# Both scaled copies of the token mixing on VectorE, and a longer TensorE delay in the list scheduler's model

## The chip, the core and the metric

The kernel runs on one core of one Trainium2 chip. The metric is the device time of one execution in microseconds, the median of three runs. TensorE multiplies matrices, VectorE and ScalarE do elementwise work, GpSimd here only writes zeros, and SyncE issues every DMA. Each of them works through its own list of instructions in order; only semaphores tie them together.

## What is computed

The reference, cut to its core: an attention with a sigmoid in place of the softmax, then a channel mixing on its output. The sizes are B = 8, 12 heads, S = 448 tokens, 64 values a head, so D = 768, and 1024 hidden values. All of it is in fp32.

```
scores = q @ k.T / sqrt(64) - log(S)
x      = sigmoid(scores) @ v                  # heads joined: (B, S, 768)
x_prev = x shifted by one token, zero in front
xk = mu_k * x + (1 - mu_k) * x_prev
xr = mu_r * x + (1 - mu_r) * x_prev
k  = relu(xk @ w_k)
out = sigmoid(xr @ w_r) * ((k * k) @ w_v)
```

## The kernel before

**Attention (lines 297 to 349).** Two heads make one tile of 128 partitions, and there are 48 tiles. Two tiles are worked on together; such a pair is called a round here, and there are 24. A round has 7 steps, one for each block of 64 keys. In a step TensorE makes a score group (`score`, line 317: eight matmul rows in the trace, into the PSUM buffer `sc`, of which there are two), ScalarE turns it into weights with one sigmoid over 128 x 896 (line 320, into `pf`, three buffers), and TensorE multiplies the weights of two steps earlier with the values (`weigh`, line 329, eight rows, into `av`). On TensorE the list runs: score group, weighing group two steps behind, next score group, and so on. A score group writes the `sc` buffer that the sigmoid of two steps earlier has read. There are four `av` banks, two for a round, so a round's banks are written again two rounds later.

**Mixing (`gather`, lines 334 to 349).** After the last weighing of a round, each of its two tiles is mixed twice, for `xr` and for `xk`. GpSimd writes the zero in front. One engine writes the scaled copy `(1 - mu) * x_prev`, reading `av`: VectorE for `xr` (line 345, `omr`), ScalarE for `xk` (line 347, `omk`). VectorE adds `mu * x` (line 348), reading `av` again, and SyncE stores the 128 x 448 result `xo`, of which there are eight buffers. A round so has two copies on VectorE, two on ScalarE and four sums on VectorE.

**Weights (lines 200 to 291).** The weights arrive as 64-bit floats, and VectorE turns them into fp32 with integer operations (lines 212 to 216), then forms the sums and differences that a seven-product (Strassen) scheme needs (line 244). For `w_r` ScalarE casts each piece into a weight slot (line 289, `slot`) and VectorE makes the remainder (line 290). This runs in the first ten rounds of the attention. The pieces of `w_k` go back to DRAM and are cast later (lines 515 and 516).

**Channel mix (lines 351 to 612).** Three linear maps, each in four halves of the tokens and seven products p, in the order 0, 1, 4, 5, 6, 2, 3. Each product is made of three partial products of high and low parts (line 530). Its operands are split by a cast on ScalarE (line 413) and a difference on VectorE (line 414), some after differences of their own (line 407). Products go to the PSUM banks `xb` (p = 0, 1, 4, 2) or `yb` (5, 6, 3); sums on VectorE read them (lines 568, 573, 574, 578, 582).

**What sets the order.** Nothing is written in engine order by hand. Every operation is handed to a `Plan` with its engine, a cost in ns, a due time and the buffers that it reads and writes. `Plan.order` then plays the engines through: an engine takes, of the operations that are ready, the one with the earliest due time. An operation is ready when those that it depends on have ended, plus `WAIT` = 170 ns, or plus 0 between two TensorE operations. `emit` issues the operations by the start times found. There are two plans, one up to the end of the attention and one for the channel mix. The scheduler's times are its own; only the order gets into the program.

Of the kernel before, what the change touches and what calls it, by code (L numbers as in the profile page):

```python
# [22 lines left out]
class Plan:  # L23
# [7 lines left out]
    def op(self, engine, cost, prio, run, reads, writes, dma=None):  # L31
        i = len(self.ops)
        deps = set()
        for r in reads:
            if r in self.writer:
                deps.add(self.writer[r])
        for w in writes:
            if w in self.writer:
                deps.add(self.writer[w])
            deps.update(self.readers.get(w, ()))  # L40
        for r in reads:
            self.readers.setdefault(r, []).append(i)
        for w in writes:
            self.writer[w] = i
            self.readers[w] = []
        deps.discard(i)
        self.ops.append(Op(engine, cost, prio, run, deps, dma))

    def order(self):
        import heapq  # L50
        ops = self.ops
        left = [len(o.deps) for o in ops]
        users = [[] for _ in ops]
        for i, o in enumerate(ops):
            for d in o.deps:
                users[d].append(i)
        at = [0.0] * len(ops)
        free, ready, waiting = {}, {}, []
        for i, o in enumerate(ops):
            free[o.engine] = 0.0  # L60
            ready.setdefault(o.engine, [])
            if not left[i]:
                heapq.heappush(waiting, (0.0, i))
        bus, start = self.bus, {}
        now = 0.0
        while len(start) < len(ops):
            while waiting and waiting[0][0] <= now:
                i = heapq.heappop(waiting)[1]
                heapq.heappush(ready[ops[i].engine], (ops[i].prio, i))
            for e in free:  # L70
                if free[e] <= now and ready[e]:
                    i = heapq.heappop(ready[e])[1]
                    o = ops[i]
                    start[i] = now
                    free[e] = now + o.cost
                    end = now + o.cost
                    if o.dma is not None:
                        bus = max(bus, end + 700) + o.dma
                        end = bus + 1300
                    for u in users[i]:  # L80
                        gap = 0 if ops[u].engine == e == "PE" else self.WAIT
                        at[u] = max(at[u], end + gap)
                        left[u] -= 1
                        if not left[u]:
                            heapq.heappush(waiting, (at[u], u))
            nxt = [free[e] for e in free if ready[e]] + ([waiting[0][0]] if waiting else [])
            if nxt:
                now = max(now, min(nxt)) if min(nxt) > now else now
        self.start = start
        return sorted(start, key=lambda i: (start[i], i))  # L90
# [8 lines left out]
def attention_then_channel_mix(  # L99
# [15 lines left out]
    nc = tc.nc  # L115
# [32 lines left out]
    xr_d = [dram.tile([P, NJ, S], F32, name=f"xr_d{b}") for b in range(B)]  # L148
# [33 lines left out]
    op = plan.op  # L182
    SP, PE, ACT, DVE, POOL = "SP", "PE", "ACT", "DVE", "POOL"
# [4 lines left out]
    def act(n, sbuf=False, ptr=False):  # L188
        return 51 + 0.834 * n + 42 * sbuf + 93 * ptr

    def dve(n, fast=False, ptr=False):
        return 69 + n / (1.92 if fast else 0.96) + 61 * ptr
# [7 lines left out]
    def dma(dst, src, prio, reads, writes):  # L200
        ns = dst.shape[0] * math.prod(dst.shape[1:]) * 4 / 300
        op(SP, 500, prio, lambda: nc.sync.dma_start(dst, src), reads, writes, dma=ns)
# [119 lines left out]
    def bank(m):  # L322
        return m % 4
# [12 lines left out]
    def gather(n, at):  # L336
        b, j = divmod(n, NP)
        x, X = av[bank(n)], ("av", bank(n))
        for mu, om, dst, key in ((mur, omr, xr_d, "xr_d"), (muk, omk, xk_d, "xk_d")):
            u = nxo[0] % len(xo)  # L340
            nxo[0] += 1
            y, Y = xo[u], ("xo", u)
            op(POOL, 200, at, lambda y=y: nc.gpsimd.memset(y[:, 0:1], 0.0), [], [Y])
            if key == "xr_d":
                op(DVE, dve(S, ptr=True), at, lambda y=y, om=om: nc.vector.tensor_scalar_mul(y[:, 1:], x[:, :S - 1], om[:, j:j + 1]), [X, ("om", key)], [Y])  # L345
            else:
                op(ACT, act(S, ptr=True), at, lambda y=y, om=om: nc.scalar.mul(y[:, 1:], x[:, :S - 1], om[:, j:j + 1]), [X, ("om", key)], [Y])  # L347
            op(DVE, dve(S, ptr=True), at, lambda y=y, mu=mu: nc.vector.scalar_tensor_tensor(y, x[:, :S], mu[:, j:j + 1], y, ALU.mult, ALU.add), [X, Y], [Y])  # L348
            dma(dst[b][:, j], y, at, [Y], [(key, n)])

# [109 lines left out]
    for t in range(T + LAG):  # L460
        n, j = t // NV * 2, t % NV
        if t < T:
            if j == 0:
                for _ in range(1 + (n % 6 == 4)):
                    convert_next(n + 4, n - 2 if n else None)
            score(n, j, t, n + j / NV)
        if t < LAG:
            continue
        n, j = (t - LAG) // NV * 2, (t - LAG) % NV
        weigh(n, j, t - LAG, n + j / NV)  # L470
        if j == NV - 1:
            for m in (n, n + 1):
                gather(m, m)
                if m + 4 < N:
                    load(m + 4, n + 0.5)
# [22 lines left out]
    op = plan.op  # L498
# [89 lines left out]
    at = 0  # L588
# [49 lines left out]
```

## Time and profile before

| | |
|---|---|
| median of three runs | 824.85 us (824.68 to 825.09) |
| the profiled execution | 824.86 us |
| its span, first to last instruction | 823.1 us |
| granted TensorE clock | 0.999 of full |
| busy: TensorE, VectorE, ScalarE | 99%, 75%, 57% of the span |
| first product of the channel mix | 263.7 us from the span's start |

The span has two parts: the attention up to 263.7 us, in which the matmuls are small and every step needs a sigmoid, and the channel mix, in which TensorE runs long products. In the profile a row gives the instructions of one kind, `x` and their count; PE is TensorE, DVE VectorE, ACT ScalarE, SPq SyncE's queue. What stands in brackets in a timeline row is the engine's idle time ahead of it and what ended that. A row with `x2` merges two instructions that follow each other.

### The profile page before, as it was taken

The numbers are of one execution on the slowest core, as the hardware profiler recorded it, in microseconds if no ns is written. First come the engines' busy times: TensorE is split into PE (matmuls) and PEld (weight loads), VectorE is DVE, ScalarE is ACT, GpSimd is POOL, SyncE is SP. The second block draws the span as 40 slices with busy tenths as digits, with TensorE's granted clock in tenths as the row PEclk, the third lists the DMA queues.
The fourth block names the chain that finished last, engine by engine and source line by source line (L and its number), as shares of the span: only waits on it lengthen the run. The fifth ranks groups of instructions, "written<-read, shape, count | busy, mean of one in ns | idle before, by whom it ended". The sixth has DMA issues, their size and how long they took to land.

```text
span 823.1 us, 15181 instructions
## 1 busy us (share of the span) xinstructions
PE 812.9 (99%) x5460; PEld 622.9 (76%) x5460; DVE 615.1 (75%) x1152; ACT 467.1 (57%) x791; POOL 10.3 (1%) x100
## 2 busy tenths in 40 slices
PE   8999999999999999999999999999999999999997
PEld 3433334343334999999999999999999999999997
DVE  0888687685654898989999639376697795977955
ACT  5788776767676553546584747647694233333320
POOL 0000000000000000000000000000000000000000
PEclk9999999999999999999999999999999999999999
DMA  8787789999872948576879542422865545755414
GB/s 274 267 312 265 268 272 317 335 352 308 287 262 90 304 161 264 169 247 206 328 228 316 195 146 102 151 96 102 288 217 188 164 145 190 225 179 178 143 39 156
DMA packets 94715, 179.80 MB, mean 218 GB/s; under 512 B 10544, under 2 KB 75312, under 8 KB 94640
## 3 DMA queue, kind: packets, MB, share of 16 engines
q1 hardware_dynamic: 94640, 178.83, 64.7%
q8 instruction: 43, 0.70, 0.4%
q14 instruction: 32, 0.26, 0.1%
HBM read 109.06 MB, written 69.73 MB: 217 GB/s over the span
## 4 chain that ended last, share of the span: by engine, by line
PE 90%; DVE 4%; ACT 2%; DMA 2%; issue 1%; SPq 0%; ACTq 0%; DVEq 0%
PE xb L530 39%; PE yb L530 29%; PE sc L317 12%; PE av L329 11%; DVE xo L348 1%; ACT pf L320 1%; DMA raw<-in_qk 1%; ACT xo L347 1%; DMA wraw<-in_moe_w_r 1%; DVE wbit L216 0%; DVE wbit L215 0%; DVE wbit L214 0%; DVE xo L345 0%; DMA wk_o<-wbit 0%; DVE wbit L244 0%
## 5 line engine op out<-in xcount | busy, mean ns | idle before, releaser
L530 PE MATMUL xb<-rra,slot 128*128 128x448 f32 x1188 | 249.8, 362 | 0.0
L530 PEld LDWEIGHTS xb<-rra,slot 128*128 128x128 f32 x1188 | 222.7, 188 | 15.5 <-issue 0.7
L530 PE MATMUL yb<-rra,slot 128*128 128x448 f32 x927 | 193.0, 362 | 0.0
L320 ACT ACTIVATE pf<-sc 128x896 f32<-128x896 f32 x168 | 152.1, 918 | 58.9 <-PE sc L317 58.8
L530 PEld LDWEIGHTS yb<-rra,slot 128*128 128x128 f32 x927 | 173.8, 187 | 11.6
L317 PE MATMUL sc<-raw 64*64 64x448 f32 x1344 | 165.6, 545 | 5.4 <-DMA raw<-in_qk 3.5
L329 PE MATMUL av<-pf,vn 64*64 64x448 f32 x1344 | 162.3, 537 | 0.0
L317 PEld LDWEIGHTS sc<-raw 64*64 64x64 f32 x1344 | 52.0, 134 | 84.9 <-issue 57.0
L329 PEld LDWEIGHTS av<-pf,vn 64*64 64x64 f32 x1344 | 54.0, 133 | 74.9 <-issue 73.6
L530 PE MATMUL xb<-rrb,slot 128*128 128x448 f32 x396 | 89.1, 362 | 0.0
L345 DVE TENSOR_SCALAR xo<-av,omr 128x447 f32<-128x447 f32 x48 | 32.5, 681 | 73.6 <-PE av L329 47.1
L413 ACT CAST rra<-ysa 128x448 fp32r<-128x448 f32 x104 | 56.6, 562 | 50.5 <-PE yb L530 21.9
L530 PEld LDWEIGHTS xb<-rrb,slot 128*128 128x128 f32 x396 | 74.2, 187 | 5.0
L414 DVE TENSOR_TENSOR rra<-ysa,rra 128x448 fp32r<-128x448 f32 x102 | 59.6, 617 | 10.4 <-ACT rra L413 10.3
L530 PE MATMUL yb<-rrb,slot 128*128 128x448 f32 x261 | 57.5, 362 | 0.0
L530 PEld LDWEIGHTS yb<-rrb,slot 128*128 128x128 f32 x261 | 48.9, 187 | 3.3
L413 ACT CAST rra<-ysb 128x448 fp32r<-128x448 f32 x58 | 31.4, 564 | 34.2 <-PE yb L530 19.2
L568 DVE TENSOR_TENSOR u<-yb,p1s 128x448 f32<-128x448 f32 x40 | 24.9, 622 | 30.5 <-PE yb L530 30.1
L566 ACT COPY p1s<-xb 128x448 f32<-128x448 f32 x40 | 21.2, 530 | 39.9 <-PE xb L530 39.5
L413 ACT CAST rra<-wbit 128x448 fp32r<-128x448 f32 x46 | 24.4, 566 | 29.7 <-PE yb L530 29.1
L414 DVE TENSOR_TENSOR rra<-ysb,rra 128x448 fp32r<-128x448 f32 x54 | 31.4, 617 | 13.0 <-ACT rra L413 13.0
L548 ACT ACTIVATE cc<-cc 128x448 f32<-128x448 f32 x48 | 27.5, 577 | 19.8 <-DVE cc L574 13.5
(59 smaller groups left out, 712.9 us busy)
## 6 DMA issues: line engine op xcount, KB each, us to landing
k_d<-cc SPq DMA_DIRECT2D x64, 224.0 KB, 2.1
raw<-in_qk SPq DMA_DIRECT2D x48, 256.0 KB, 4.1
vn<-in_v SPq DMA_DIRECT2D x48, 224.0 KB, 5.3
xr_d<-xo SPq DMA_DIRECT2D x48, 224.0 KB, 3.5
xk_d<-xo SPq DMA_DIRECT2D x48, 224.0 KB, 3.4
r_d<-cc SPq DMA_DIRECT2D x48, 224.0 KB, 2.0
out<-cc SPq DMA_DIRECT2D x48, 224.0 KB, 3.1
raw<-in_qk SPq DMA_DIRECT2D x48, 192.0 KB, 4.5
```

What stands on the lines that cost most here:

```text
L317: nc.tensor.matmul(u[half[h ^ (m % 2)], m % 2, :S], x[half[h], c], x[half[h], D:D + S], start=True, stop=True)
L320: op(ACT, act(2 * S), at, lambda: nc.scalar.activation(f, u[:, :, :S], AF.Sigmoid, bias=NEG_LOG_S, scale=SCALE), [("sc", t % 2)], [("pf", ...
L329: nc.tensor.matmul(av[bank(m)][half[r ^ (m % 2)], :S], vn[m % RAW][half[r], j, :], pf[t % PFB][half[r], m % 2, :], start=j == 0, stop=j == ...
L345: op(DVE, dve(S, ptr=True), at, lambda y=y, om=om: nc.vector.tensor_scalar_mul(y[:, 1:], x[:, :S - 1], om[:, j:j + 1]), [X, ("om", key)], [Y])
L347: op(ACT, act(S, ptr=True), at, lambda y=y, om=om: nc.scalar.mul(y[:, 1:], x[:, :S - 1], om[:, j:j + 1]), [X, ("om", key)], [Y])
L348: op(DVE, dve(S, ptr=True), at, lambda y=y, mu=mu: nc.vector.scalar_tensor_tensor(y, x[:, :S], mu[:, j:j + 1], y, ALU.mult, ALU.add), [X, ...
L413: op(ACT, act(TB, True), at, lambda t=t: nc.scalar.copy(hi[t], y[:, t]), [Y[t]], [H[t]])
L414: op(DVE, dve(TB), at, lambda t=t: nc.vector.tensor_sub(lo[t], y[:, t], hi[t]), [Y[t], H[t]], [L[t]])
L530: nc.tensor.matmul(bank, a, b, start=first and t == 0 and e == 0, stop=t == n - 1 and e == 2, skip_group_check=True)
L548: op(ACT, act(TB), at, lambda: nc.scalar.activation(c, src, AF.Relu), R, [C])
L566: op(ACT, act(TB), at, lambda: nc.scalar.copy(p1s[i], x), [X], [P1])
L568: op(DVE, dve(TB), at, lambda: add(u2[i], y, p1s[i]), [Y, P1], [U2])
```

## The change

It has two parts. In `gather` the scaled copy for `xk` goes to VectorE as well, so that both copies are made there and ScalarE makes none. In `Plan.order` the delay from a TensorE operation to one on another engine becomes 370 ns; all others stay at 170, and 0 between TensorE operations.

```diff
                     for u in users[i]:
-                        gap = 0 if ops[u].engine == e == "PE" else self.WAIT
+                        gap = 0 if ops[u].engine == e == "PE" else self.WAIT + 200 * (e == "PE")
                         at[u] = max(at[u], end + gap)
...
             op(POOL, 200, at, lambda y=y: nc.gpsimd.memset(y[:, 0:1], 0.0), [], [Y])
-            if key == "xr_d":
-                op(DVE, dve(S, ptr=True), at, lambda y=y, om=om: nc.vector.tensor_scalar_mul(y[:, 1:], x[:, :S - 1], om[:, j:j + 1]), [X, ("om", key)], [Y])
-            else:
-                op(ACT, act(S, ptr=True), at, lambda y=y, om=om: nc.scalar.mul(y[:, 1:], x[:, :S - 1], om[:, j:j + 1]), [X, ("om", key)], [Y])
+            op(DVE, dve(S, ptr=True), at, lambda y=y, om=om: nc.vector.tensor_scalar_mul(y[:, 1:], x[:, :S - 1], om[:, j:j + 1]), [X, ("om", key)], [Y])
             op(DVE, dve(S, ptr=True), at, lambda y=y, mu=mu: nc.vector.scalar_tensor_tensor(y, x[:, :S], mu[:, j:j + 1], y, ALU.mult, ALU.add), [X, Y], [Y])
```

TensorE's and GpSimd's lists stay the same, row for row. On VectorE, ScalarE and SyncE instructions change places. In the changed kernel line numbers from 345 on are three lower: the copies are line 344, the sums 345, the operand splits 410 and 411, the slot additions 513, the sums of products 570, 571 and 575.

VectorE, the first round's mixing, before (`xo` are the mixed rows, `omr` and `omk` the two 1 - mu, `mur` and `muk` the two mu, `wbit` and `wexpo` the weight conversion that follows):

```order
L345 TENSOR_SCALAR xo0_156<-av0_135,omr_65 128x447
L345 TENSOR_SCALAR xo2_158<-av1_136,omr_65 128x447
L348 SCALAR_TENSOR_TENSOR xo0_156<-av0_135,mur_63,xo0_156 128x448
L348 SCALAR_TENSOR_TENSOR xo1_157<-av0_135,muk_64,xo1_157 128x448
L348 SCALAR_TENSOR_TENSOR xo2_158<-av1_136,mur_63,xo2_158 128x448
L348 SCALAR_TENSOR_TENSOR xo3_159<-av1_136,muk_64,xo3_159 128x448
L212 TENSOR_SCALAR wbit_127<-wraw_126 128x384
```

The same place now:

```order
L344 TENSOR_SCALAR xo0_156<-av0_135,omr_65 128x447
L344 TENSOR_SCALAR xo1_157<-av0_135,omk_66 128x447
L345 SCALAR_TENSOR_TENSOR xo0_156<-av0_135,mur_63,xo0_156 128x448
L345 SCALAR_TENSOR_TENSOR xo1_157<-av0_135,muk_64,xo1_157 128x448
L344 TENSOR_SCALAR xo2_158<-av1_136,omr_65 128x447
L344 TENSOR_SCALAR xo3_159<-av1_136,omk_66 128x447
L345 SCALAR_TENSOR_TENSOR xo2_158<-av1_136,mur_63,xo2_158 128x448
L345 SCALAR_TENSOR_TENSOR xo3_159<-av1_136,muk_64,xo3_159 128x448
L212 TENSOR_SCALAR wbit_127<-wraw_126 128x384
```

The two copies for `xk` stand among VectorE's own, and one tile is finished before the other is begun.

ScalarE, the first casts of weight pieces, in the second and third round, before (`pf` are the sigmoids, `slot` the cast pieces):

```order
L320 ACTIVATE pf1_154<-sc1_140 128x896
L289 CAST slot6_122<-wbit_127 128x384
L320 ACTIVATE pf2_155<-sc0_139 128x896
L289 CAST slot2_118<-wbit_127 128x384
L320 ACTIVATE pf0_153<-sc1_140 128x896
L347 ACTIVATE xo5_161<-av2_137,omk_66 128x447
L347 ACTIVATE xo7_163<-av3_138,omk_66 128x447
L320 ACTIVATE pf1_154<-sc0_139 128x896
```

The same place now, as far as the casts of the following round:

```order
L320 ACTIVATE pf2_155<-sc0_139 128x896
L289 CAST slot6_122<-wbit_127 128x384
L289 CAST slot2_118<-wbit_127 128x384
L320 ACTIVATE pf0_153<-sc1_140 128x896
...
L320 ACTIVATE pf2_155<-sc0_139 128x896
L289 CAST slot0_116<-wbit_127 128x384
L320 ACTIVATE pf0_153<-sc1_140 128x896
L289 CAST slot3_119<-wbit_127 128x384
L289 CAST slot4_120<-wbit_127 128x384
L320 ACTIVATE pf1_154<-sc0_139 128x896
L289 CAST slot1_117<-wbit_127 128x384
```

The copies are gone, and the first two casts stand together behind one sigmoid, one sigmoid later than the first of them stood.

VectorE, the product p = 6 in the last half of the first linear map, before (`cc` are the sums that read the banks `yb` and `xb`, `slot` an addition for the next map's weights, `rra` and `ysa` operands):

```order
L573 TENSOR_TENSOR cc4_2485<-yb0_2494,p1s0_2473 128x448
L414 TENSOR_TENSOR rra_124<-ysa_125,rra_124 128x448
L574 TENSOR_TENSOR cc4_2485<-xb0_2498,cc4_2485 128x448
L573 TENSOR_TENSOR cc0_2481<-yb1_2495,p1s1_2474 128x448
L516 TENSOR_TENSOR slot2_118<-wc2_2488,slot2_118 128x384
L574 TENSOR_TENSOR cc0_2481<-xb1_2499,cc0_2481 128x448
```

The same place now:

```order
L570 TENSOR_TENSOR cc4_2485<-yb0_2494,p1s0_2473 128x448
L411 TENSOR_TENSOR rra_124<-ysa_125,rra_124 128x448
L571 TENSOR_TENSOR cc4_2485<-xb0_2498,cc4_2485 128x448
L404 TENSOR_TENSOR ysa_125<-ysb_2472,ysa_125 128x448
L513 TENSOR_TENSOR slot2_118<-wc0_2486,slot2_118 128x384
L513 TENSOR_TENSOR slot2_118<-wc1_2487,slot2_118 128x384
L570 TENSOR_TENSOR cc0_2481<-yb1_2495,p1s1_2474 128x448
L570 TENSOR_TENSOR cc1_2482<-yb2_2496,p1s2_2475 128x448
L571 TENSOR_TENSOR cc0_2481<-xb1_2499,cc0_2481 128x448
```

A difference and two slot additions stand between the first row's sums and the second row's, which then wait behind the third row's first sum.

## The prediction

> **What bounds the kernel now.** I read the page first, for the busiest engine.
>
> ```profile
> PE 812.9 (99%) x5460; PEld 622.9 (76%) x5460; DVE 615.1 (75%) x1152; ACT 467.1 (57%) x791; POOL 10.3 (1%) x100
> ```
>
> TensorE is busy for 812.9 of 823.1 us, so the change can only pay or cost through TensorE's own schedule. A busy row hides stretched groups, so next I read the chain of waits in order of time. Its pieces give the start and length of TensorE's groups: `sc` is a score group, `xb` and `yb` are the products of the channel mix.
>
> ```profile
> 34.64 0.75 PE sc L317 x8
> ...
> 46.40 0.75 PE sc L317 x8
> ...
> 69.70 0.75 PE sc L317 x8
> ...
> 95.66 0.80 PE sc L317 x8
> ...
> 111.41 0.75 PE sc L317 x8
> ...
> 201.61 0.80 PE sc L317 x8
> ...
> 217.03 0.75 PE sc L317 x8
> ...
> 247.10 0.85 PE sc L317 x8
> ...
> 263.73 16.41 PE xb L530 x81
> 280.14 10.80 PE yb L530 x54
> ...
> 811.14 7.22 PE yb L530 x36
> ```
>
> One step is a score group and a weighing group. From 111.41 to 201.61 there are 60 steps in 90.20 us, 1.5033 us each, with no stall. The other distances are whole steps plus a loss: 34.64 to 46.40 is 7 steps and 1.24 us; to 69.70 is 15 steps and 0.75; to 95.66 is 17 and 0.40; to 111.41 is 10 and 0.72; 201.61 to 217.03 is 10 and 0.39; to 247.10 is 20 and nothing, but that row is 0.85 long, 0.10 over. From 263.73 to 818.36 (811.14 + 7.22) the products follow each other; what stands behind, 4.7 us, is the last sums and the last store.
>
> Who held the late score groups shows in the timeline of ScalarE. `pf` is the sigmoid that TensorE waits for, `xo` a scaled copy, `slot` a weight cast; the brackets hold the idle time before a row and what ended it.
>
> ```profile
> 26.04 0.92 ACT L320 ACTIVATE pf<-sc 128x896 f32<-128x896 f32 x1 [0.59 <-PE sc L317]
> ...
> 30.89 1.16 ACT L347 ACTIVATE xo<-av,omk 128x447 f32<-128x447 f32 x2 [0.40 <-DVE xo L345]
> ...
> 34.02 0.92 ACT L320 ACTIVATE pf<-sc 128x896 f32<-128x896 f32 x1 [0.35 <-PE sc L317]
> ...
> 41.34 0.91 ACT L320 ACTIVATE pf<-sc 128x896 f32<-128x896 f32 x1
> 42.58 1.22 ACT L347 ACTIVATE xo<-av,omk 128x447 f32<-128x447 f32 x2 [0.33 <-DVE xo L345]
> 43.70 0.91 ACT L320 ACTIVATE pf<-sc 128x896 f32<-128x896 f32 x1
> ...
> 64.45 1.16 ACT L347 ACTIVATE xo<-av,omk 128x447 f32<-128x447 f32 x2 [0.54 <-DVE xo L345]
> ...
> 91.95 1.11 ACT L289 CAST slot<-wbit 128x384 fp32r<-128x384 f32 x2 [0.91 <-DVE wbit L216]
> ...
> 106.86 0.91 ACT L320 ACTIVATE pf<-sc 128x896 f32<-128x896 f32 x1
> ...
> 108.69 0.93 ACT L320 ACTIVATE pf<-sc 128x896 f32<-128x896 f32 x1
> ...
> 213.28 1.16 ACT L347 ACTIVATE xo<-av,omk 128x447 f32<-128x447 f32 x2 [0.86 <-DVE xo L345]
> ...
> 223.79 1.16 ACT L347 ACTIVATE xo<-av,omk 128x447 f32<-128x447 f32 x2 [0.46 <-DVE xo L345]
> 224.84 1.72 ACT L320 ACTIVATE pf<-sc 128x896 f32<-128x896 f32 x2
> ...
> 244.94 1.16 ACT L347 ACTIVATE xo<-av,omk 128x447 f32<-128x447 f32 x2 [0.56 <-DVE xo L345]
> ```
>
> 26.04 to 34.02 is 5 steps and 0.46 us, behind the copies at 30.89. So the losses after the start sum to 0.46 + 1.24 + 0.75 + 0.40 + 0.72 + 0.39 + 0.10 = 4.06 us. Copies alone stand ahead of 0.46, 0.75 (64.45), 0.39 (213.28) and 0.10 (244.94); casts alone ahead of 0.40 (91.95). In the two mixed stretches the sigmoids on both sides of a copy pair are 2.36 (41.34 to 43.70) and 1.83 us apart (106.86 to 108.69), that is 0.86 and 0.33 over a step; the rest, 0.38 and 0.39, is casts. Copies: 2.89 us. Casts: 1.17 us.
>
> Why only some copy pairs cost anything shows in a quiet round, with TensorE's rows of the same moment.
>
> ```profile
> 224.37 0.93 PE L317 MATMUL sc<-raw 64*64 64x448 f32 x8
> ...
> 225.87 0.93 PE L317 MATMUL sc<-raw 64*64 64x448 f32 x8
> ```
>
> The sigmoid at 224.84 takes 0.92 and ends at 225.76; the score group that reuses its buffer starts at 225.87, on time. Its own score group, a step before the one at 224.37, ended near 223.80 (222.87 + 0.93), so it was 1.04 late and had 0.11 left: the margin is some 1.1 us, an ordinary copy pair eats nearly all of it, and whatever else delays ScalarE there becomes a TensorE stall.
>
> **The copies.** Each of the 24 rounds has two copies on ScalarE and two on VectorE; the former move to the latter. A round's mixing on VectorE, and rows that a later step uses:
>
> ```profile
> 18.81 0.68 DVE L345 TENSOR_SCALAR xo<-av,omr 128x447 f32<-128x447 f32 x1 [7.14 <-PE av L329]
> 20.72 0.68 DVE L345 TENSOR_SCALAR xo<-av,omr 128x447 f32<-128x447 f32 x1 [1.22 <-ACT xo L347]
> ...
> 23.68 0.36 DVE L212 TENSOR_SCALAR wbit<-wraw 128x384 uint32<-128x384 uint32 x1
> ...
> 29.71 0.56 DVE L290 TENSOR_TENSOR slot<-wbit,slot 128x384 fp32r<-128x384 f32 x1 [0.66 <-ACT slot L289]
> ...
> 35.05 0.35 DVE L212 TENSOR_SCALAR wbit<-wraw 128x384 uint32<-128x384 uint32 x1
> ...
> 37.26 0.55 DVE L216 SCALAR_TENSOR_TENSOR wbit<-wexpo,wbit 128x384 f32<-128x384 uint32 x1
> ```
>
> It took from 18.81 to 23.68, 4.87 us: six instructions, 0.592 us apart (23.68 less 20.72, over the last five), and 1.22 us of waiting for ScalarE's copy out of the same `av` bank. Now eight instructions by 0.592 make 4.74 us and wait for no copy elsewhere. The bounds of the moved copy are its two neighbours, 0.592 apart here and at most 0.68 if each had to wait for the one before it to end, 5.44 us a round. I take 0.592, since a sum stands two places behind the copy that it reads, and that copy has then ended (0.68 against 1.18). All waits for ScalarE's copies, us and times:
>
> ```profile
>   ACT xo L347: 25.2, 21
> ```
>
> 48 added copies by 0.59 are 28.4 us; 25.2 us of waiting goes. VectorE's load is as good as unchanged and ScalarE loses its copies, so the copies' 2.89 us of stalls go whole; at 0.68 a copy and a sum, VectorE would be 0.57 us a round slower than now, which the 10.5 us between two rounds cover. What is late next is the casts.
>
> **The casts and the longer delay.** TensorE's order is the same in every row. On the others the delay moves single instructions. At the first conversions two casts now stand together behind one sigmoid, and VectorE needs their results (L290) ahead of its second mixing. Undisturbed, that sigmoid starts at 29.05 (26.04 and two steps) and ScalarE is free 0.80 later (224.84: two in 1.72, the last 0.92). The casts end near 30.9; VectorE starts the mixing near 31.4, is through at 36.1, and has the next piece to cast 2.76 later (35.05 to 37.81), at 38.9. ScalarE comes to that cast at 37.4 (26.04, seven steps, 0.80), waits 1.5 us, and starts the next sigmoid near 39.3, 1.2 late against 38.07: a stall of 0.2 to 0.3. The next two casts hang on the same VectorE chain, each behind a sum that follows the last cast's: some 0.5. What is left of the lag may cost 0.1 at the casts of the first operand. The later conversions start without that lag, because a round has 10.52 us (7 steps) for 4.74 of mixing, so I take nothing for them. Estimate for all casts after: 0.85 us; bounds none, and twice the 1.17 of now.
>
> The stores of the mixed rows and the memsets on GpSimd stay, and SyncE's queue has the same order up to 100 us; behind that single stores move by a few rows. The page has a load's time from issue to landing at its end:
>
> ```profile
> raw<-in_qk SPq DMA_DIRECT2D x48, 256.0 KB, 4.1
> ```
>
> I cost the moves at nothing, as a load is asked for about a round, 10.5 us, ahead of its use and lands in 4.1 us; a round without that cover would cost up to 4.1 us.
>
> **The channel mix.** There TensorE could only lose, being gapless. Rows of VectorE, then of TensorE:
>
> ```profile
> 270.46 1.70 DVE L414 TENSOR_TENSOR rrb<-ysa,rrb 128x448 fp32r<-128x448 f32 x3 [1.74 <-ACT rrb L413]
> ...
> 402.86 0.62 DVE L574 TENSOR_TENSOR cc<-xb,cc 128x448 f32<-128x448 f32 x1
> ```
>
> ```profile
> 404.18 5.16 PE L530 MATMUL xb<-rra,slot 128*128 128x448 f32 x25
> ```
>
> The first operand made after the attention is ready at 272.16, 8 us before its product (280.14), so TensorE may arrive 3 us earlier. The tightest bank is `xb` of the first linear map: read until 403.48, written again at 404.18, 0.70 us. In the new order the first of these reads comes sooner and the second row's later, behind two additions for weight slots; I take zero, with 0 to 0.5 us in each of the four halves as bounds.
>
> **Sum.** The profiled execution took 824.86 us, 823.1 of it span; the median is 824.85, so no correction. 824.86 - 4.06 + 0.85 = 821.65, say 821.7. Bounds of this case: 820.8 (no cast stall) and 823.1 (cast stalls of 2.34).
>
> **The rivals.**
> - *Casts take the place of the copies.* ScalarE has fifteen spots with casts; if ten hold their sigmoid as the 0.40 at 91.95 did, the time is 824.86 - 4.06 + 4.0 = 824.8. For it: ScalarE works in order, and casts wait for VectorE. Against it: most stand where ScalarE now has slack. 0.08.
> - *The banks of the channel mix.* Four times 0.5 us given back: 823.7. For it: the 0.70; against: the slack of all other products. 0.04.
> - *VectorE becomes the bound: slower.*
>
> ```profile
> 18.80:110.00 91.20, 89.42 (x934) 35.61 (x930) 74.82 (x149) 71.99 (x104) 3.64 (x32) 1.00 0.82 278
> ```
>
> In the first nine rounds VectorE is busy 74.82 of 91.2 us. Eighteen more copies by 0.59 make 85.4; 5.8 are left, and the `av` ring bears a lag of another 5.8 (10.52 less 4.74). If in-order waits for casts cost VectorE w in each round, TensorE loses 9w - 11.6 us. It decides from w = 1.74, where 820.8 + 9w - 11.6 passes 824.86; at w = 2 it gives 827.2. Against it: the wait for a cast at 29.71 was 0.66, and the waits for copies go. 0.05. [...]
> - *The change doesn't do what it says:* the stalls are TensorE's own or come from the loads and stay. 824.9. Against it: the 60 steps from 111.41 have the same TensorE rows and the same loads, no casts, and lose nothing. 0.03.
>
> **Numbers.** Forecast 821.7, chance 0.80. The range adds the bank rival above, and 0.2 below for the spread of runs (824.68 to 825.09): 820.6 to 823.7. It leaves out 0.16 of the rivals' chance. About 0.2%, 1.65 us, is what a measurement can tell from no change. Faster, under 823.2: 0.80. Same: casts, banks, nothing done, 0.08 + 0.04 + 0.03 = 0.15. Slower: 0.05.
>
> **What would show it.** Right: no wait of VectorE for ScalarE's copies; a mixing of 4.7 us; no stall from 49 us on in the attention; the first `xb` product near 260.5 instead of 263.7; products gapless from there, and 4.7 us at the end. Wrong: score groups longer than 0.75 us in the chain behind casts beyond the first conversions, a mixing that starts over 5 us after its weighing, or gaps between products around 280 to 415 us.

## The result, and the profile after

| | before | changed |
|---|---|---|
| median of six runs | 824.8 us (824.45 to 825.09) | 820.41 us (819.95 to 821.99) |
| profiled execution, and its span | 824.86 us, 823.1 us | 820.3 us, 818.5 us |

The changed kernel takes 0.9949 of the time, with an interval of 0.9936 to 0.9962: it is faster by some 4.4 us. The forecast was 821.7, its range began at 820.6, and the median lies 0.2 us below that. One execution of a kernel further down, of 915.67 us at a granted clock of 0.85, is left out of all numbers.

The busy times on the page of after, and the shares of the chain that ended last:

```profile
PE 810.3 (99%) x5460; PEld 691.9 (85%) x5460; DVE 640.7 (78%) x1200; ACT 444.6 (54%) x743; POOL 9.7 (1%) x100
...
PE 99%; DMA 0%; DVE 0%; issue 0%
```

VectorE has gained 25.6 us of work and ScalarE has lost 22.5, yet the whole chain is now TensorE. The same chain in order of time (start, length, what) shows where the end came forward:

```profile
3.49 5.18 PE sc L317 x24
...
256.72 2.25 PE av L329 x24
258.98 16.40 PE xb L527 x81
275.38 10.80 PE yb L527 x54
...
361.79 5.59 PE xb L527 x27
367.38 5.40 PE yb L527 x27
...
806.58 7.21 PE yb L527 x36
```

No late score group stands between the start and 256.72. The channel mix begins at 258.98 in place of 263.73, 4.75 us earlier; one product in it, at 361.79, is 0.19 us longer than its 5.40; the last one ends at 813.79, and 4.7 us follow, as before.

VectorE's waits up to 262 us (what waited, for what: us, times, longest):

```profile
DVE xo L344 <- PE av L329: 40.5, 15, 6.2
...
DVE slot L290 <- ACT slot L289: 2.2, 4, 0.8
```

There is no wait for a copy on ScalarE any more. The timeline of VectorE, over the first two rounds' mixing:

```profile
18.24 0.68 DVE L344 TENSOR_SCALAR xo<-av,omr 128x447 f32<-128x447 f32 x1 [6.17 <-PE av L329]
...
22.98 0.36 DVE L212 TENSOR_SCALAR wbit<-wraw 128x384 uint32<-128x384 uint32 x1
...
28.17 1.03 DVE L290 TENSOR_TENSOR slot<-wbit,slot 128x384 fp32r<-128x384 f32 x2 [0.49 <-ACT slot L289]
29.12 0.68 DVE L344 TENSOR_SCALAR xo<-av,omr 128x447 f32<-128x447 f32 x1
...
33.85 0.35 DVE L212 TENSOR_SCALAR wbit<-wraw 128x384 uint32<-128x384 uint32 x1
```

A mixing takes 4.74 us (18.24 to 22.98), and 4.73 the second time. The timeline of ScalarE, at the first casts:

```profile
25.32 0.92 ACT L320 ACTIVATE pf<-sc 128x896 f32<-128x896 f32 x1 [0.59 <-PE sc L317]
26.82 0.92 ACT L320 ACTIVATE pf<-sc 128x896 f32<-128x896 f32 x1 [0.59 <-PE sc L317]
27.64 0.91 ACT L289 CAST slot<-wbit 128x384 fp32r<-128x384 f32 x2
28.45 0.92 ACT L320 ACTIVATE pf<-sc 128x896 f32<-128x896 f32 x1
29.83 0.92 ACT L320 ACTIVATE pf<-sc 128x896 f32<-128x896 f32 x1 [0.46 <-PE sc L317]
...
36.67 0.51 ACT L289 CAST slot<-wbit 128x384 fp32r<-128x384 f32 x1
37.35 0.92 ACT L320 ACTIVATE pf<-sc 128x896 f32<-128x896 f32 x1 [0.17 <-PE sc L317]
38.16 0.92 ACT L289 CAST slot<-wbit 128x384 fp32r<-128x384 f32 x2
```

The sigmoid at 28.45 is 0.13 late (26.82 and 1.50), and the next is on time. The cast at 36.67 waits for nothing. So the casts cost nothing either, where 0.85 was forecast. ScalarE's waits ahead of casts in the attention show why (what waited, for what: us, times, longest). Before:

```profile
ACT slot L289 <- DVE wbit L216: 5.4, 6, 1.4
```

After:

```profile
ACT slot L289 <- DVE wbit L244: 0.2, 1, 0.2
```

Counted in sigmoids, 16 of the 21 casts stand one or more later in the new order, and there the pieces that they read are ready.

That is not all of it: 824.86 less the 4.06 us of stalls gives 820.80, and this execution has a gap of 0.19 on top, yet took 820.3. The rest lies in the first 9 us. One row of the view by stretches from each kernel, 6 to 9 us; behind TensorE's 3.00 busy us stands its number of matmul rows, and the third figure from the end is its granted clock. Before:

```profile
6.00:9.00 3.00, 3.00 (x18) 1.25 (x18) 0.00 (x0) 1.79 (x2) 0.00 (x0) 1.00 1.03 369
```

After:

```profile
6.00:9.00 3.00, 3.00 (x24) 1.58 (x24) 0.00 (x0) 1.90 (x3) 0.00 (x0) 1.00 1.00 322
```

TensorE was busy all the time in both, and did 18 matmul rows in one and 24 in the other. The first matmul rows of both executions last 0.95 to 1.0 us, the later ones 0.54. The 1.00 for the clock says nothing about this phase: the clock records kept with the two traces begin only at 9.16 us (before) and 7.80 us (after), at full clock, and the view prints 1.00 where there is no record. The first rows of 0.54 us start within 0.1 us of these two moments. So the phase ended earlier in the profile of after: its third score group was through at 8.67 (3.49 + 5.18), before's at 9.39, with its last two rows:

```profile
8.54 0.85 PE L317 MATMUL sc<-raw 64*64 64x448 f32 x2
```

That is 0.72 us which the change has nothing to do with, as the next section shows.

### The profile page after: what moved, and what is told of

The parts are those of the page before. It is cut to its first block, busy times and chain, and to the rows that moved or that the text cites. A ratio compares the mean times of both kernels' runs of the same rounds, so it can differ in the third digit from the quotient of the medians.

```text
span 818.5 us, 15170 instructions
## 1 busy us (share of the span) xinstructions
PE 810.3 (99%) x5460; PEld 691.9 (85%) x5460; DVE 640.7 (78%) x1200; ACT 444.6 (54%) x743; POOL 9.7 (1%) x100
## 4 chain that ended last, share of the span: by engine, by line
PE 99%; DMA 0%; DVE 0%; issue 0%
PE xb L527 39%; PE yb L527 29%; PE sc L317 16%; PE av L329 15%; DMA raw<-in_qk 0%; DVE cc L579 0%; DVE cc L552 0%
## 5 line engine op out<-in xcount | busy, mean ns | idle before, releaser
L320 ACT ACTIVATE pf<-sc 128x896 f32<-128x896 f32 x168 | 154.0, 917 | 89.9 <-PE sc L317 89.7
L317 PE MATMUL sc<-raw 64*64 64x448 f32 x1344 | 198.4, 542 | 3.5 <-DMA raw<-in_qk 3.5
L329 PE MATMUL av<-pf,vn 64*64 64x448 f32 x1344 | 195.9, 536 | 0.0
L317 PEld LDWEIGHTS sc<-raw 64*64 64x64 f32 x1344 | 89.0, 134 | 45.6 <-DMA raw<-in_qk 5.3
L329 PEld LDWEIGHTS av<-pf,vn 64*64 64x64 f32 x1344 | 88.7, 133 | 40.3 <-ACT pf L320 0.4
L410 ACT CAST rra<-ysb 128x448 fp32r<-128x448 f32 x58 | 31.4, 565 | 34.2 <-PE yb L527 19.2
L411 DVE TENSOR_TENSOR rra<-ysb,rra 128x448 fp32r<-128x448 f32 x54 | 31.4, 625 | 13.4 <-ACT rra L410 13.4
```

Source lines behind the costliest of these rows:

```text
L317: nc.tensor.matmul(u[half[h ^ (m % 2)], m % 2, :S], x[half[h], c], x[half[h], D:D + S], start=True, stop=True)
L320: op(ACT, act(2 * S), at, lambda: nc.scalar.activation(f, u[:, :, :S], AF.Sigmoid, bias=NEG_LOG_S, scale=SCALE), [("sc", t % 2)], [("pf", ...
L329: nc.tensor.matmul(av[bank(m)][half[r ^ (m % 2)], :S], vn[m % RAW][half[r], j, :], pf[t % PFB][half[r], m % 2, :], start=j == 0, stop=j == ...
L410: op(ACT, act(TB, True), at, lambda t=t: nc.scalar.copy(hi[t], y[:, t]), [Y[t]], [H[t]])
L411: op(DVE, dve(TB), at, lambda t=t: nc.vector.tensor_sub(lo[t], y[:, t], hi[t]), [Y[t], H[t]], [L[t]])
```

## The experiments

The theory: TensorE's stalls came from ScalarE's copies and casts; with the copies on VectorE both kinds are gone, because ScalarE no longer waits for VectorE inside a round. The rivals: the longer delay did it; ScalarE's sheer load did it; the extra is a matter of the start. "The changed kernel" is the one predicted; unless a sentence says otherwise, an experiment is an edit of it. Results of work that was only added are not used.

The profiled executions of all kernels can be laid beside each other by three numbers: when the third score group ends, what TensorE loses in late score groups after it (the excess of each distance between the ends of score groups over 1.503 us), and gaps in the channel mix. What is left of the time is the same everywhere:

| kernel | profiled us | third score group ends | late groups | gaps | rest |
|---|---|---|---|---|---|
| before | 824.86 | 9.39 | 4.03 | 0 | 811.44 |
| changed | 820.30 | 8.67 | 0 | 0.19 | 811.44 |
| e0, changed again | 820.32 | 8.89 | 0 | 0 | 811.43 |
| e1, copies only | 821.06 | 9.48 | 0.15 | 0 | 811.43 |
| e2, delay only | 823.07 | 8.17 | 3.49 | 0 | 811.41 |
| e4, late casts | 821.73 | 9.58 | 0.72 | 0 | 811.43 |
| e5, load on ScalarE | 820.73 | 9.00 | 0.28 | 0 | 811.45 |
| e6, all copies on ScalarE | 833.82 | 8.00 | 14.40 | 0 | 811.42 |
| e7, load on VectorE | 828.03 | 8.19 | 7.87 | 0.52 | 811.45 |
| e8, six early matmuls | 819.85 | 8.44 | 0 | 0 | 811.41 |
| e9, four early matmuls | 819.38 | 7.96 | 0 | 0 | 811.42 |
| e10, copies only again | 820.79 | 9.23 | 0.12 | 0 | 811.44 |

So the change's own gain is the 4.03 us of late groups (4.06 as the prediction read them from rounded rows). The gap of 0.19 did not come back, and the starts run from 8.00 to 9.58 in kernels whose first rows are the same.

**The changed kernel once more (e0).** No edit.

> The changed kernel once more, for the start. In its profile TensorE's matmuls ran at half speed (0.95 us each in place of 0.54) until 7.2 us, in the profile of before until 8.5 us, and this made 0.7 us of the difference between the two. Theory (chance): the moment at which TensorE comes to full speed differs between executions of one and the same program, so this profile may have the third score group end anywhere from 8.6 to 9.4 us; time 820.0 to 822.0. Rival (the change makes it): the start is that of the first profile to 0.1 us, with the third score group ending at 8.7 us.

Measured: 820.34 us (820.03 to 820.52), ratio 0.9949 (0.9936 to 0.9963). No late score group, no gap; the start is neither before's nor that of the first profile. The gap and the start belong to the execution.

**The copies alone (e1).** The longer delay is taken back:

```diff
-                        gap = 0 if ops[u].engine == e == "PE" else self.WAIT + 200 * (e == "PE")
+                        gap = 0 if ops[u].engine == e == "PE" else self.WAIT
```

> Both copies on VectorE, the delay in the scheduler's model back at 170 ns for all. Theory (the copies pay for all, the longer delay costs a little): attention as in the changed kernel, without one late score group; all products of the channel mix at 5.40 us in a group of 27, so without the 0.19 us that one group of the changed kernel lost; time 0.2 us under the changed kernel's. Rival (the longer delay orders the casts better and earns the 1.17 us of the casts): late score groups behind casts, 0.5 to 1.2 us over the changed kernel.

Measured: 820.48 us (819.99 to 821.06), ratio 0.9952 (0.9939 to 0.9964). The order in the attention is the changed kernel's on every engine, but for one operand difference on VectorE, at 239.98 us here and at 264.39 us there; the channel mix differs. No group is late but one of 0.15 next to the start. Whether the delay costs the expected 0.2 us in the channel mix can't be seen against the spread. The copies bring the whole gain, that of the casts included.

**The delay alone (e2).** ScalarE keeps its copies:

```diff
-            op(DVE, dve(S, ptr=True), at, lambda y=y, om=om: nc.vector.tensor_scalar_mul(y[:, 1:], x[:, :S - 1], om[:, j:j + 1]), [X, ("om", key)], [Y])
+            if key == "xr_d":
+                op(DVE, dve(S, ptr=True), at, lambda y=y, om=om: nc.vector.tensor_scalar_mul(y[:, 1:], x[:, :S - 1], om[:, j:j + 1]), [X, ("om", key)], [Y])
+            else:
+                op(ACT, act(S, ptr=True), at, lambda y=y, om=om: nc.scalar.mul(y[:, 1:], x[:, :S - 1], om[:, j:j + 1]), [X, ("om", key)], [Y])
```

> The longer delay alone, the copies for xk still on ScalarE. Theory (the copies pay for all): the late score groups of before stay, 4 us in all, time 824.4 to 825.2, within 0.05% of before. Rival (the delay pays): the casts' 1.2 us or more go, 823.6 or less.

Measured: 824.09 us (823.07 to 825.0, 11 runs), ratio 0.9992 (0.9983 to 1.0001). The late groups stand where they stood, 3.49 us of them; the one that lost 0.85 before loses 0.35, and the last one, of 0.10, is gone. The casts stand behind the same sigmoids as before, so it is the moved copies that put them later in the changed kernel. The delay is no cause of the gain; a half microsecond of its own is possible and not shown.

**The casts one step later (e4).** In the prediction's walk the first two casts came behind the sigmoid one step after the one behind which they really stand. Here they are put there: the next score group and its sigmoid are issued ahead of them.

```diff
     def emit(self, late=None):
         line = self.order()
+        if late is not None:
...
+            part = line[first:stop]
+            pe = [i for i in part if ops[i].engine == "PE"]
+            line[first:stop + 1] = pe + [s] + [i for i in part if i not in pe]
...
```

> The changed kernel with one sigmoid and its score group put ahead of the first two weight casts on ScalarE, so that these casts stand where the prediction had wrongly put them, one step (1.5 us) later than the scheduler has them. Theory (the prediction's walk was right but for that place): VectorE's second mixing starts 1.3 to 1.6 us later, the cast of the next round waits for VectorE, and TensorE loses 0.3 us at that sigmoid and some 0.5 at the next, 0.8 in all over the changed kernel. Rival (the walk was wrong elsewhere too, or the margin of 1.1 us takes it up): at most 0.2 us lost.

Measured: 821.1 us (820.06 to 821.73), ratio 0.9955 (0.9943 to 0.9968). The time alone tells nothing here; the trace does. ScalarE's timeline (its lines are ten higher, L299 is the cast, L330 the sigmoid):

```profile
29.23 0.92 ACT L330 ACTIVATE pf<-sc 128x896 f32<-128x896 f32 x1 [0.59 <-PE sc L327]
30.05 0.91 ACT L299 CAST slot<-wbit 128x384 fp32r<-128x384 f32 x2
...
36.75 0.92 ACT L330 ACTIVATE pf<-sc 128x896 f32<-128x896 f32 x1 [0.59 <-PE sc L327]
39.07 0.51 ACT L299 CAST slot<-wbit 128x384 fp32r<-128x384 f32 x1 [1.40 <-DVE wbit L226]
39.48 0.91 ACT L330 ACTIVATE pf<-sc 128x896 f32<-128x896 f32 x1
40.29 1.16 ACT L299 CAST slot<-wbit 128x384 fp32r<-128x384 f32 x2
41.36 0.91 ACT L330 ACTIVATE pf<-sc 128x896 f32<-128x896 f32 x1
```

Now the third cast waits 1.40 us for VectorE, where the walk had 1.5, and the sigmoid behind it is 1.23 late (39.48 against 36.75 and 1.50), where it had 1.2. Three score groups lose 0.28, 0.38 and 0.06 us, where it had 0.2 to 0.3, some 0.5, and 0.1. The walk was sound and its starting place wrong.

**Load on ScalarE without the waits (e5).** 48 copies go back to ScalarE's places, but between spare places of SBUF, so that they read no `av` bank and wait for no copy on VectorE. VectorE makes all the real ones.

```diff
...
+            if key == "xk_d":
+                op(ACT, act(S, ptr=True), at, lambda u=u, om=om: nc.scalar.mul(junk[1 + u // 2 % 2][:, 1:], junk[0].bitcast(F32)[:, :S - 1], om[:, j:j + 1]), [X, ("om", key)], [("junk", u // 2 % 2)])
```

> The changed kernel, with 48 extra copies on ScalarE in the place where the copies for xk stood before; they read and write spare SBUF instead of an av bank, so they wait for nobody, and their results are not used. Theory (it was the wait for VectorE's copy out of the same bank that carried a copy pair over the margin; the work alone fits in ScalarE's idle time): sigmoids behind the extra pairs 0.4 to 0.6 us late, no late score group there, time within 0.4 us of the changed kernel, 820.0 to 820.8. Rival (the work itself cost the 2.9 us): 823 or more, with score groups late behind the pairs.

Measured: 820.57 us (820.11 to 820.73), ratio 0.9948 (0.9936 to 0.9961). ScalarE's timeline in a quiet round (L349 is the added pair):

```profile
218.35 0.92 ACT L323 ACTIVATE pf<-sc 128x896 f32<-128x896 f32 x1 [0.59 <-PE sc L320]
219.17 1.21 ACT L349 ACTIVATE slot<-slot,omk 128x447 fp32r<-128x447 f32 x2
220.28 0.90 ACT L323 ACTIVATE pf<-sc 128x896 f32<-128x896 f32 x1
221.36 0.92 ACT L323 ACTIVATE pf<-sc 128x896 f32<-128x896 f32 x1 [0.17 <-PE sc L320]
```

The pair is as long as the old one (1.21; before, 1.16) and stands in the same place, but it starts at once; the sigmoid is 0.43 late (220.28 against 218.35 and 1.50) and no group behind a pair loses anything. So the late score groups came from the time that a copy waited ahead of a sigmoid, 0.33 to 0.86 us in the rows of before, and not from ScalarE's work alone: only the two together went past what a score group can bear. ScalarE's copy and VectorE's read one `av` bank in turns and write different `xo` buffers. In the trace of before ScalarE's copies wait for VectorE's 16 times, 9.3 us, and VectorE's for ScalarE's 21 times, 25.2 us. e5's copies, which read no `av` bank, start at once behind a sigmoid (219.17), and in e6, where ScalarE makes all four copies of a round, they stand 0.52 us apart with no wait between them. So the waits were there only where both engines had copies that read one bank; what puts such reads in turn, no run shows.

**All copies on ScalarE (e6).**

```diff
-            op(DVE, dve(S, ptr=True), at, lambda y=y, om=om: nc.vector.tensor_scalar_mul(y[:, 1:], x[:, :S - 1], om[:, j:j + 1]), [X, ("om", key)], [Y])
+            op(ACT, act(S, ptr=True), at, lambda y=y, om=om: nc.scalar.mul(y[:, 1:], x[:, :S - 1], om[:, j:j + 1]), [X, ("om", key)], [Y])
```

> Both kinds of copy on ScalarE, four in a row in each round, with the longer delay. Theory (margin of 1.1 us): four copies take 2.1 us and none waits for a copy on VectorE, so the sigmoid behind them is some 1.5 us late and TensorE loses about 0.4 us in each of 24 rounds, 10 us in all: 829 to 832. Rival (only waits for the bank matter, work on ScalarE is free): 822 or less.

Measured: 834.18 us (833.0 to 834.72), ratio 1.0113 (1.0098 to 1.0129): slower than before. ScalarE's timeline in a round without casts:

```profile
218.57 0.92 ACT L320 ACTIVATE pf<-sc 128x896 f32<-128x896 f32 x1 [0.59 <-PE sc L317]
219.38 0.63 ACT L344 ACTIVATE xo<-av,omr 128x447 f32<-128x447 f32 x1
...
220.93 0.65 ACT L344 ACTIVATE xo<-av,omk 128x447 f32<-128x447 f32 x1
221.44 1.75 ACT L320 ACTIVATE pf<-sc 128x896 f32<-128x896 f32 x2
```

Four copies, 0.52 us apart and with no wait, put the sigmoid 1.37 late (221.44 against 218.57 and 1.50), and the score group loses 0.47. So the margin, counted from the sigmoid's undisturbed start, is 0.90 us. The 1.1 that the prediction read from one quiet round is counted from the end of the score group; from the undisturbed start (222.42 and 1.50) that round's sigmoid, at 224.84, was 0.92 late with no score group late behind it, so the two agree. Nineteen rounds lose 0.45 to 0.50 each (0.4 was expected); where casts add to the copies a group loses up to 1.40, which the expectation didn't have, and the total is 14.4 in place of 10.

**Load on VectorE (e7).** The slower rival, put to the test: each round has four more copies on VectorE, 2.37 us (4 x 0.592).

```diff
...
+            op(DVE, dve(S, ptr=True), at, lambda u=u, om=om: nc.vector.tensor_scalar_mul(junk[1 + u % 2][:, 1:], x[:, :S - 1], om[:, j:j + 1]), [X, ("om", key)], [("junk", u % 2)])
```

> The changed kernel with four more copies in each round on VectorE, out of the same av banks into spare SBUF, unused: 2.37 us a round. This is the slower rival's place: by its formula the nine first rounds lose 9 x 2.37 - 11.6 = 9.7 us, 830. Theory (the scheduler lets the mixing go ahead of the weight conversions, which have 250 us, and these move back in the order): late score groups of 0.5 us in all at most, 820.0 to 821.0.

Measured: 828.85 us (827.86 to 829.68), ratio 1.0048 (1.0036 to 1.0061). The view by stretches, two parts of the attention (length, then busy us of TensorE, weight loads, VectorE, ScalarE), with the wait of TensorE's weighing groups:

```profile
18.00:110.00 92.00, 92.00 (x984) 66.74 (x980) 91.88 (x176) 64.30 (x82) 4.17 (x34) 1.00 0.83 271
110.00:266.40 156.40, 150.03 (x1583) 75.32 (x1575) 155.87 (x282) 94.09 (x108) 6.25 (x54) 1.00 0.82 280
```

```profile
PE av L331 <- DVE xo L348: 6.4, 4, 1.8
```

And the same view of the changed kernel:

```profile
18.00:110.00 92.00, 92.00 (x986) 62.74 (x982) 86.78 (x173) 66.47 (x89) 3.81 (x35) 1.00 0.86 288
110.00:259.00 149.00, 149.00 (x1587) 101.03 (x1579) 111.69 (x193) 91.62 (x102) 5.41 (x53) 1.00 0.83 286
```

VectorE is busy for 198.47 of 241 us in the changed kernel, so 42.5 us were free, and 56.9 us (24 x 2.37) were added. Now it is full, and TensorE waits for its sums at the first weighing of four rounds after 110 us, 6.4 us by the waits; the late groups lose 7.87 us in all. The theory forecast 0.5 us at most: it fell. The rival's formula, 9w - 11.6 us, gives 9.7 at w = 2.37 and was near in size, but not in place: the first nine rounds lose nothing, since the order lets weight conversions slip into later ones (up to 110 us VectorE does some 68 rows of conversion in place of 101), and the debt is paid there.

**Matmuls ahead of the first loads (e8, e9, and e10 beside it).** If the length of the first rows hangs on what TensorE did before, matmuls of zeros while the first load is on its way should help. e8 has six of them in the changed kernel, e9 four in e1; e10 is e1 again.

```diff
+    hot = slots[0][:, 2 * NJH * HN:2 * NJH * HN + P].bitcast(F32)
+    nc.vector.memset(hot, 0.0)
...
+    for _ in range(4):
+        nc.tensor.matmul(av[3][:, :112], hot, hot[:, :112], start=True, stop=True)
```

> The changed kernel with six small matmuls on zeros (128 x 128 by 112 columns, results not used) ahead of the first score group, in the 2.5 us in which TensorE waits for the first load. Theory (TensorE comes to full speed a time of some 4 us after it begins to work): full speed at 5 to 6.5 us in place of 7 to 9.8, third score group at 7.9 to 8.4 us, time 0.3 to 1.2 us under the changed kernel's. Rival (full speed comes at a moment that the work does not set, or the loads bound the start): third score group at 8.6 us or later, same time.

> The kernel with the copies on VectorE and the old delay, and four matmuls of zeros (128x128 by 112 columns, results unused) ahead of the first score group, which end about when the first loads land at 3.5 us. Theory (earlier work brings the half-length matmul rows earlier): 0.3 to 1.0 us under the same kernel without them, first score group still at 3.5, third score group done by 8.4 or before in the profile. Rival (the moment of the half-length rows is not set by what TensorE has done): same time within 0.3 us, and a third score group that ends anywhere in the 8.0 to 9.6 us seen so far.

> The kernel with the copies on VectorE and the old delay once more, beside the one with four early matmuls on the same chip. Both theories: 820.5, within 0.4 of its first run's 820.48, no late score group in the attention; the end of its third score group gives one more sample of the start (8.0 to 9.6 us so far).

Measured: e8 819.85 us (819.3 to 820.55), ratio 0.9940 (0.9928 to 0.9953); e9 819.61 (819.38 to 820.61), 0.9948 (0.9934 to 0.9961); e10 819.38 to 820.79 in four runs, 0.9949 (0.9936 to 0.9963). In e8 the six end too late and push the first score group to 3.91. In e9 they fit, as TensorE's timeline shows (four matmuls are eight rows):

```profile
1.08 2.05 PE L184 MATMUL av<-slot 128*128 128x112 f32 x8 [1.08 <-DVE slot L164]
3.57 4.40 PE L321 MATMUL sc<-raw 64*64 64x448 f32 x24 [0.44 <-DMA raw<-in_qk]
```

Its third score group ends at 7.96 (3.57 + 4.40), the earliest of all, but the others reach 8.00 without help, and two of e9's five runs are at 820.5. The ten runs with early matmuls have a median of 819.73 us, the twenty without them, of the changed kernel and of the copies alone, one of 820.41. That points to 0.7 us; the two kernels run side by side overlap, so it is not shown. The two traces don't show it either: their clock records begin 3.6 us (e8) and 2.7 us (e9) after the first score row, where those of the ten executions without early matmuls begin 2.7 to 6.1 us after it.

Not tried: another size of the delay, and more runs of e9 and e10 to settle the 0.7 us.

## Why the prediction was right or wrong

**Right.** TensorE's late score groups were the whole price, and nothing took their place. The copies' 2.89 us went whole, and so did the casts' 1.17; that the 4.06 divide in this way is a reading of the trace of before, which no run tests by itself. The mixing takes 4.74 us, as worked out from eight instructions by 0.592, and VectorE waits for no copy. In the first nine rounds it is busy for 86.78 of 92.0 us, where 85.4 of 91.2 was forecast. The moved loads and stores cost nothing. The channel mix is gapless but for 0.19 us in one of the changed kernel's two profiled executions. That the change does nothing is ruled out by e1, and the banks give nothing back.

**The step that failed** is in the part on the casts: "Undisturbed, that sigmoid starts at 29.05 (26.04 and two steps)". It is one step: the casts stand behind the sigmoid `pf2`, the next after the row at 26.04, as the order's own rows said. In the trace of after, the row that answers to 26.04 is 25.32, and the casts follow the sigmoid at 26.82. With 1.50 us counted too many, VectorE's second mixing was put near 31.4; it came at 29.12, 2.28 us earlier: 0.72 is the earlier start, and the other 1.56 is about the one step. From that lag came the 0.2 to 0.3, the 0.5 and the 0.1 that made up the 0.85 us. e4 puts the casts where the prediction had them and gets those stalls, 0.72 us in all; where they really stand, they cost nothing. So the bound that the prediction called "no cast stall", 820.8, was the case itself. The first product of the channel mix shows the same: 260.5 was forecast and 258.98 measured, and the 0.85 of the casts with the 0.72 of the start makes up the difference.

**The term that was not in the sum** is the start. At before's own start the changed kernel takes 811.43 + 9.39 = 820.82, the bound again. But the ten profiled executions without early matmuls end their third score group at 8.00 to 9.58, with a median of 8.95, and before's profile, from which the sum was made, had one of the late ones. A typical start gives 820.4, which is the median that was measured. So 0.4 us of the difference from the forecast come from the one execution that the sum was made from, which is chance and not the change. The 0.2 us that the range added for the spread came from three runs; later runs of before reach from 823.75 to 826.24.

**The rivals.** Casts in the copies' place: none of them held a score group. VectorE as the bound: it is a real limit, but 42.5 us of its time in the attention are still free, and e7 had to add 56.9 to go over it, which makes the kernel slower than before. The rival's price was near what e7 measured; its place, the first nine rounds, was wrong.

## What to carry to other kernels

Where two engines read one PSUM bank in turns, look at what the waiting engine has behind it: here a pair of copies was affordable on either engine, and the waits of 0.3 to 0.9 us between them, in front of an instruction with 0.9 us of margin, were the cost. When a cost is derived by walking an order step by step, fix the first step against a row of the order and a row of the trace, since every later number inherits its error. Before the last half microsecond of a sum is argued, take the start of several executions: the sum of one profile is only as typical as its start.

## What the hardware showed

The phase of long matmul rows was not expected to differ between executions. The first row of 0.54 us starts 2.9 to 6.3 us after the first matmul in the ten executions without early matmuls, with 14 to 28 rows of 0.7 to 1.0 us before it. The clock records kept with these traces begin, at full clock, 2.7 to 6.1 us after the first matmul (4.31 in the changed kernel's first profile, 5.65 in before's) and within 0.3 us of that row; a second record, behind the last matmul, reads 0.5. Ahead of the first record no clock is kept, and the views print 1.00 there all the same. In the traces of the changed kernel, of before and of e6 the stretch at full clock is a whole number of steps of 3.413 us: 237 of them are 808.96 us in the changed kernel, 238 are 812.37 us in before, 242 are 826.02 us in e6. The spread of the start, 3.4 us, is as long as one such step.

What sets the moment of the full clock, no run shows. Whether earlier matmuls bring it forward, the traces of e8 and e9 don't show, with the full clock 6.4 and 5.2 us after their first early matmul; the medians, 819.73 us with early matmuls and 820.41 without, point that way, and it stays open.
